# Two query buffers, loaded two tiles ahead, and a planner that counts 330 instead of 230 GB/s for transfers

## The chip, the cores and the metric

The kernel runs on one core of a Trainium2 chip. The metric is the device time of one execution in microseconds (us). The core has TensorE for matrix products (PE in the profile, its weight loads PEld), VectorE (DVE), ScalarE (ACT), GpSimd (POOL), and SyncE (SP), whose queue here issues nearly all DMA transfers. Each engine takes its own instructions strictly in the order in which the program was written out, and waits at the head of its queue until what it needs is there.

## What is computed

```python
# q, k, v: (4, 8, 576, 64); f: (4, 8, 576)
scores = q @ k.T / sqrt(64) + cum[:, :, :, None] - cum[:, :, None, :]   # cum = cumsum(log(clip(f)))
attn = softmax(where(causal, scores, -1e9)) @ v
x = attn as (2304, 512)
h = x @ w_in                                    # 512 x 1024
solu = h * softmax(h)
x = layernorm(solu) * g_ln @ w_out              # 1024 x 512
h = relu(x @ w2_in)                             # 512 x 2048
out = (h * h) @ w2_out                          # 2048 x 512
```

## The kernel before

**Precision.** Products are made from two halves: each float32 operand is split into a rounded part and a remainder (names ending in h and l), and three matmuls replace one.

**Attention with the first layer.** There are 20 query tiles (4 batches, 5 tiles each, of 128 or 64 rows). For each tile `load_k`, `load_q` and `load_v` fetch the rows from memory. `prep_k` and `prep_q` turn them into operands: for queries, three instructions for each of two halves j, on ACT, DVE or POOL (line 378, 380 or 384 for the scaled copies, line 541 on DVE for the remainder). The finished query operands Q1 and Q2 have two buffers, picked by tile number. The raw keys have two buffers KN (one for each half), the raw values six, and the raw queries one, `QN`, of 512 columns; a tile `q3` of 640 columns stands unused until the second layer's weights are put there. For each of 160 heads follow the scores (line 576, PE), the minimum (lines 594 and 597, DVE), the exponential (line 611, ACT), transposes (line 630, PE), their copies out (line 376 or another, by engine), and the product with the values (line 650). When a block of 128 tokens is complete, `first` runs the first layer on it (lines 869 to 950) and `out1` its second product (lines 820 to 822).

**Weights.** `convert` loads a piece of a weight as 64-bit words (line 715) and rebuilds float32 values with ACT, DVE and POOL (lines 729 to 747). The pieces of w_in are staged in four buffers, those of w_out in two (`xc` and `ws`). In `early2` the second layer's weights pass through five buffers called `free`, where they are converted and combined on POOL or DVE (lines 1098 and 1106), and are written to scratch memory: `w2d` (line 758), `w2u` (line 1101), `w2f` (line 1114). A buffer is used again only when its write has landed.

**Second layer.** `half_up` (line 1341), `unit` (line 1392) and `step` (lines 1497 to 1499) run the two big products. Their weights are read from the scratch memory by `within` (line 1168) and by `weights` in `unit` (line 1381).

**The order.** Nothing of this order is written by hand. `Plan.add` collects steps with a cost in ns for each engine that may run them, a due time (`prio`), and the buffers they read and write. `Plan.lay` then plays the program through at the time of building: a list scheduler with one server for each of PE, DVE, ACT and POOL, and one server called dma for all transfers. A transfer takes its stated cost on that server, one after the other, and then 1,410 to 1,790 ns until an engine sees it (`LAT`). At each point the scheduler takes what can start first, among those within 20 ns what is due first, and on engines other than PE it holds back for a more urgent step in some cases (`DUE`, `WORTH`). The order found is the order of the program; its times are not used on the chip, where each engine waits for what it needs. Costs in the code: 1,140 ns for 256 KB of queries, keys or values, 4.45 ns per column for a piece of a first-layer or raw second-layer weight (2,278 ns for 512 KB), 350 ns for the 16 KB rows of line 506, 570 ns for a write of 128 KB, `LOAD2` = 900 ns for 256 KB of the second layer's prepared weights. Where PE would wait for more than 400 ns in the first 140 us, `fill` puts transposes of no use there, so that TensorE's clock stays up (line 1706 in the trace).

In the loop over tiles the loads are added so (before):

```python
if h == PQ and n + 1 < NQ:        # PQ = 6
    prep_q(n + 1, when[s])
    if n + 2 < NQ:
        load_q(n + 2, when[s])
```

Of the kernel before, what the change touches and what calls it, by code (L numbers as in the profile page):

```python
# [27 lines left out]
class Plan:  # L28
# [11 lines left out]
        dve=dict(pe=230, dve=127, act=198, pool=203, dma=1230),  # L40
        act=dict(pe=110, dve=142, act=153, pool=160, dma=1234),
        pool=dict(pe=135, dve=75, act=75, pool=88, dma=1200),
        dma=dict(pe=1500, dve=1450, act=1410, pool=1450, dma=1790),
# [16 lines left out]
    def add(self, eng, fn, prio, reads=(), writes=(), take=None, uses=(), late=0, port=False, kind="r"):  # L60

        s = Step()
        s.eng, s.fn, s.prio, s.take, s.no, s.late = eng, fn, prio, take, len(self.steps), late
        deps = {}
        s.uses = tuple(uses) + ((take,) if take else ())
        for k in s.uses:  # L70
            self.users.setdefault(k, []).append(s)
        s.weak, s.port, s.kind = None, port, kind
        for k in reads:
            if k in self.writer:
                deps[self.writer[k].no] = self.writer[k]
            rs = self.readers.setdefault(k, [])
            if k in self.banks or k[0] in ("pp", "hp"):

                if rs and rs[-1].no not in deps:
                    s.weak = rs[-1]  # L80
                    deps[s.weak.no] = s.weak
            rs.append(s)
        for k in writes:
            if k in self.writer:
                deps[self.writer[k].no] = self.writer[k]
            for r in self.readers.get(k, ()):
                deps[r.no] = r
        for k in writes:
            self.writer[k] = s
            self.readers[k] = []  # L90
        deps.pop(s.no, None)
        s.deps = list(deps.values())
        s.succ = []
        for d in s.deps:
            d.succ.append(s)
        s.left = len(s.deps)
        s.rdy = {}
        s.end = None
        self.steps.append(s)
        return s  # L100
# [26 lines left out]
    def lay(self, slack=60):  # L127
# [53 lines left out]
        while todo:  # L181
            pick = None
            for e in engs:
                cand = []
                for s in avail[e]:
# [5 lines left out]
                    if e == "dve" and len(s.eng) > 1:  # L191

                        o = min(max(free[x], s.rdy[x]) + s.eng[x] for x in s.eng if x != e)
                        if t + s.eng[e] + SHIFT > o:
                            continue
# [73 lines left out]
def tile_kernel(ctx: ExitStack, tc: tile.TileContext, q, k, v, f, w_in, w_out, g_ln, w2_in, w2_out, out):  # L269
    nc = tc.nc  # L270
    NT, DM = out.shape
# [4 lines left out]
    P = 128  # L276
# [16 lines left out]
    HH = H // 2  # L293
# [17 lines left out]
    def new(tag, shape, dt=F32):  # L311

        tags[tag] = sb.tile([P] + list(shape), dt, tag=tag, name=f"{tag}_{len(tags)}")
        return tags[tag]
# [5 lines left out]
    woh, wol = (new(t, [KF, DM], F32R) for t in ("woh", "wol"))  # L320

    K2 = [new(f"k2{j}", [HH, KW], F32R) for j in range(2)]
    QN = new("qn", [DM])
    VN = [new(f"vn{i}", [DM]) for i in range(NV)]
    KN = [new(f"kn{i}", [DM]) for i in range(2)]
    pt = new("pt", [NPT * 5 * P])
# [4 lines left out]
    scratch = new("free", [5 * 768])  # L331
    new("ws", [768])
    new("xc", [768])
    new("q3", [640])
    new("xw", [256])
    ADJ = [new(f"adj{i}", [AW]) for i in reversed(range(NADJ))][::-1]
    ST = [new(f"st{i}", [2]) for i in range(NST)]
# [32 lines left out]
    def copy(n, dst, src, prio, reads, writes, uses=(), scale=None, psum=True, only=None):  # L370

        def fn():
            x = 1.0 if scale is None else scale
            if s.on == "act":
                if scale is None:
                    nc.scalar.copy(dst(), src())  # L376
                else:
                    nc.scalar.activation(out=dst(), in_=src(), func=AF.Copy, scale=scale)
            elif s.on == "pool":
                nc.gpsimd.tensor_scalar(out=dst(), in0=src(), scalar1=x, scalar2=1.0, op0=ALU.mult, op1=ALU.mult)  # L380
            elif scale is None:
                nc.vector.tensor_copy(dst(), src())
            else:
                nc.vector.tensor_scalar(out=dst(), in0=src(), scalar1=scale, scalar2=None, op0=ALU.mult)

        ap = not (scale is None or isinstance(scale, float))
        ns = dict(act=(51 if psum else 94) + 0.833 * n + (93 if ap else 0))
        ns["dve"] = 67 + 1.042 * n if psum else 68 + 0.522 * n + (61 if ap else 0)
        if not psum:
            ns["pool"] = (244 if ap else 161) + 0.833 * n  # L390
        if only:
            ns = {e: ns[e] for e in only}
        s = pl.add(ns, fn, prio, reads, writes, uses=uses, port=not psum)
        return s
# [10 lines left out]
    NQ = len(tiles)  # L405
# [22 lines left out]
    when = []  # L428
# [19 lines left out]
    def load_k(n, prio):  # L448
        T = tiles[n]
        m, o = T["m"], HH * T["q0"]  # L450
        for j in range(2):
            pl.add(
                dict(dma=1140 * m / P),
                lambda j=j: nc.sync.dma_start(KN[j][:, 0 : HH * m], k[T["b"], j, :, o : o + HH * m]), prio + 2 * j,
                writes=[("kn", j)],
            )

    def load_q(n, prio):
        T = tiles[n]
        m, o = T["m"], HH * T["q0"]  # L460
        pl.add(
            dict(dma=1140 * m / P), lambda: nc.sync.dma_start(QN[:, 0 : HH * m], q[T["b"], :, o : o + HH * m]), prio + 1,
            writes=["qn"],
        )

    def load_v(n, prio):
        b, t = tiles[n]["b"], tiles[n]["t"]
        vslot[b, t] = n % NV


        def fn():
            nc.sync.dma_start(VN[n % NV], v[b, t * P : t * P + P])

        pl.add(dict(dma=1140), fn, max(prio + 4, V0), writes=[("vn", n % NV)])
# [51 lines left out]
    def prep_q(n, prio):  # L526
        m = tiles[n]["m"]
        i = n % 2
        raw = QN[:, 0 : HH * m].rearrange("p (h s) -> p h s", s=m)
        for j, src in enumerate(own):  # L530
            q1, q2 = Q1[i][j], Q2[i][j]
            if n == 0 and j:
                prio = SECOND
            for rows, dst, nm in ((LO, q2, "qh"), (HI, q1, "qd")):
                copy(
                    HH * m, lambda rows=rows, dst=dst: dst[rows, :, 0:m], lambda src=src: raw[src], prio + 2 * j, ["qn"],
                    [(nm, i, j)], (), SC, False, None if n else ("act", "dve")[j:] if j else ("act",),
                )

            def lo(src=src, q1=q1, hi=(q1 if j else q2)):  # L540
                nc.vector.scalar_tensor_tensor(
                    out=q1[LO, :, 0:m], in0=raw[src], scalar=SC, in1=hi[src, :, 0:m].bitcast(F32), op0=ALU.mult,
                    op1=ALU.subtract,
                )

            pl.add(
                dict(dve=67 + 1.045 * HH * m), lo, prio + 2 * j, ["qn", ("qd" if j else "qh", i, j)], [("ql", i, j)],
                port=True,
            )

# [416 lines left out]
    def k_keys(nm, j):  # L967
        cs = ("kh",) if nm == "k1" else ("ka0", "ka1", "kl")
        return [c for y in cs for c in kcells(y, j, 0, KW)]

    held = {f"{nm}{j}": k_keys(nm, j) for nm in ("k1", "k2") for j in range(2)}
    for i in range(NV):
        held[f"vn{i}"] = [("vn", i)]
    for i in range(2):
        held[f"kn{i}"] = [("kn", i)]
        for j in range(2):
            held[f"q1{i}{j}"] = [("ql", i, j), ("qd", i, j)]
    held["qn"], held["q3"] = ["qn"], []
    for i in range(NADJ):
        held[f"adj{i}"] = [("adj", i, y) for y in range(2)]  # L980
    held["pt"] = [("pt", i, g) for i in range(NPT) for g in range(5)]
# [372 lines left out]
    def unit(b, p, prio):  # L1354
# [70 lines left out]
        prod(3, prio)  # L1425
        copy(TB, u2f, lambda: half(0), prio, [ks[0]], [uk], slots_of([ks[0]]))
        add(u2f, u2f, 1, prio, [], [uk])
        r1, r2 = new_r(*s1, prio), new_r(*s2, prio)
        c22, c12, c11, c21 = rof(*s2, 2, 2), rof(*s2, 0, 2), rof(*s1, 0, 2), rof(*s1, 2, 2)
        add(c22, u2f, 2, prio, [uk, "rqs"], [r2], (), r2)  # L1430
        add(c22, c22, 3, prio, [], [r2], [r2])
        prio += MID
        for i in (4, 5, 6):
# [122 lines left out]
    pl.add(dict(dma=350), sync(fl, f.rearrange("b h s -> (b h) s")), -9e6, [], ["f"])  # L1556
    load_k(0, -8e6)
    load_q(0, -8e6)
    load_v(0, -8e6)
    ones = E[0 : B * H, P : P + S]  # L1560
# [9 lines left out]
    for y, (a, e) in enumerate(((0, P), (P, S))):  # L1570
        w = slice(a, e)
        n = e - a
# [76 lines left out]
    for n in range(NQ):  # L1649
        for h in range(H):  # L1650
            s = n * H + h
            if h == 0 and n + 2 < NQ:
                load_v(n + 2, when[s])
            if h == PK and n + 1 < NQ:
                prep_k(n + 1, when[s])
                if n + 2 < NQ:
                    load_k(n + 2, when[s])
            if h == PQ and n + 1 < NQ:
                prep_q(n + 1, when[s])
                if n + 2 < NQ:  # L1660
                    load_q(n + 2, when[s])
            head(s)
            w = 4 if n >= QUADS else 2
            if (h + 1) % w == 0:
                mix(s, w)
        if tiles[n]["done"]:
            first(tiles[n]["x"])
# [9 lines left out]
    for x in ORDER:  # L1677
        nm, p = x[0], int(x[1])
# [10 lines left out]
    for b in range(1, NTB // 2 + 1):  # L1689
        for p in range(KP):  # L1690
            n = (b - 1) * KP + p
# [22 lines left out]

SHIFT = 650
XB = 1
AHEAD = 10000.0
V0, LOAD1 = -15000.0, 3000.0  # L1720
# [74 lines left out]
```

## Time and profile before

| | |
|---|---|
| time, median of 3 runs | 811.17 us (811.07 to 811.35) |
| profiled execution, span from first to last instruction | 811.2 us |
| PE busy | 790.8 us, 97% |
| PEld busy | 726.7 us, 90% |
| DVE busy | 638.9 us, 79% |
| ACT busy | 550.3 us, 68% |
| POOL busy | 384.6 us, 47% |
| moved by DMA | 159.69 MB, mean 197 GB/s |

The profiled execution has only its span of 811.2 us as a time of its own. Busy is the share of time in which an engine had an instruction in work; matmuls are pipelined and their ends are modelled, so a busy PE isn't a PE at its peak, and the filler transposes count as busy too.

### The profile page before, as it was taken

The page shows a single profiled execution, that of the slowest core. Times are in us where ns is not written, and L with a number is a line of the kernel's source. Part 1 is how long each engine was busy: PE and PEld are TensorE (multiplying, and loading weights), DVE is VectorE, ACT ScalarE, POOL GpSimd, SP SyncE. Part 2 cuts the span into 40 slices and gives each one's busy share as a digit, 9 for nine tenths or more (in the row PEclk, how much of TensorE's full clock was granted, in tenths as well). Part 3 has the DMA queues.
Part 4 walks back from the last instruction along what each step waited for, and adds up shares of the span by engine and source line. Part 5 has one row for each costly group of instructions (what it writes and reads, how often), then busy time and mean ns, then how long its engine had stood idle before and what let it go on. Part 6 is the DMA issues. An engine that isn't in the chain of part 4 may idle for free.

```text
span 811.2 us, 19134 instructions
## 1 busy us (share of the span) xinstructions
PE 790.8 (97%) x6607; PEld 726.7 (90%) x6607; DVE 638.9 (79%) x1627; ACT 550.3 (68%) x1425; POOL 384.6 (47%) x520
## 2 busy tenths in 40 slices
PE   7899999999999999999999999999999999999997
PEld 6677788888888888888989999999999999999997
DVE  8788788787786667886677879779778877987777
ACT  6899998889998888898886775445335343533442
POOL 6467778666778686777757622120211121112110
PEclk9999999999999999999999999999999999999999
DMA  6644346656664555665477899696767767675401
GB/s 216 206 117 140 105 128 186 206 173 190 199 206 163 189 171 165 196 229 180 169 247 232 265 309 368 213 321 212 229 207 233 230 203 223 216 232 186 159 1 53
DMA packets 109665, 159.69 MB, mean 197 GB/s; under 512 B 12832, under 2 KB 52768, under 8 KB 109568
## 3 DMA queue, kind: packets, MB, share of 16 engines
q1 hardware_dynamic: 109280, 158.21, 60.9%
q8 instruction: 52, 0.85, 0.4%
q14 instruction: 45, 0.37, 0.2%
q10 hardware_dynamic: 288, 0.26, 0.1%
HBM read 121.65 MB, written 36.72 MB: 195 GB/s over the span
## 4 chain that ended last, share of the span: by engine, by line
PE 47%; POOL 2%; DVE 2%; issue 1%; DMA 1%; ACT 1%; DVEq 0%; POOLq 0%
PE z L1392 9%; PE pp L1392 9%; PE hp L1497 4%; PE hp L1498 4%; PE hp L1499 4%; PE z L1341 3%; PE xo L1498 2%; PE xo L1499 2%; PE xo L1497 2%; DMA w2d<-free 1%; PE pp L1498 1%; PE pp L1499 1%; PE pp L1497 1%; PE pp L820 1%; PE pp L822 1%
## 5 line engine op out<-in xcount | busy, mean ns | idle before, releaser
L611 ACT ACTIVATE adj<-z,st 64x288 f32<-64x288 f32 (+9 forms) x192 | 95.0, 498 | 17.7 <-DVE st L597 15.9
L576 PE MATMUL z<-k,q 80*64 80x288 f32 (+17 forms) x384 | 89.9, 331 | 0.2
L597 DVE CUSTOM_DVE_ANT_0 z<-z,maskb 128x128 f32<-128x128 f32 (+8 forms) x144 | 65.3, 462 | 26.8 <-PE z L576 24.8
L630 PE MATMUL pp<-ident,adj 128*128 128x128 f32 (+1 forms) x480 | 76.4, 273 | 9.2 <-ACT adj L611 8.2
L821 PE MATMUL pp<-ln,wol 128*128 128x256 f32 x288 | 80.1, 278 | 0.0
L822 PE MATMUL pp<-ln,woh 128*128 128x256 f32 x288 | 80.1, 278 | 0.0
L630 PEld LDWEIGHTS pp<-ident,adj 128*128 128x128 f32 (+1 forms) x480 | 50.7, 140 | 32.4 <-ACT adj L611 22.4
L376 ACT COPY pt<-pp 128x384 f32<-128x384 f32 (+5 forms) x167 | 67.5, 422 | 15.2 <-PE pp L630 13.7
L1153 DVE TENSOR_TENSOR k<-adj,k 128x512 fp32r<-128x512 f32 (+1 forms) x71 | 48.9, 688 | 32.5 <-POOL k L380 25.2
L743 POOL TENSOR_TENSOR free<-free 128x256 uint32<-128x256 uint32 x64 | 49.1, 772 | 33.9 <-DVE free L737 20.7
L576 PEld LDWEIGHTS z<-k,q 128*128 128x128 f32 (+3 forms) x384 | 54.9, 176 | 8.3 <-ACT adj L611 4.1
L869 PE MATMUL hp<-wih,xl 128*128 128x512 f32 x144 | 60.0, 417 | 0.8 <-ACT hp L908 0.8
L650 PE MATMUL xo<-pt,vn 128*64 128x128 f32 (+1 forms) x960 | 60.4, 268 | 0.1
L650 PEld LDWEIGHTS xo<-pt,vn 128*64 128x64 f32 x960 | 48.6, 137 | 9.4 <-issue 5.4
L870 PE MATMUL hp<-wil,xh 128*128 128x512 f32 x144 | 56.6, 393 | 0.2 <-DVE wil L747 0.2
L871 PE MATMUL hp<-wih,xh 128*128 128x512 f32 x144 | 56.8, 394 | 0.0
L1106 POOL TENSOR_TENSOR free<-free 128x256 f32<-128x256 f32 x64 | 52.5, 821 | 7.5 <-DMA w2d<-free 4.8
L821 PEld LDWEIGHTS pp<-ln,wol 128*128 128x128 f32 x288 | 54.4, 189 | 0.4
L822 PEld LDWEIGHTS pp<-ln,woh 128*128 128x128 f32 x288 | 54.1, 188 | 0.0
L1098 POOL TENSOR_TENSOR free<-free 128x256 fp32r<-128x256 f32 x63 | 50.0, 805 | 7.4 <-ACT free L376 6.9
L380 POOL TENSOR_SCALAR k<-adj 128x512 fp32r<-128x512 f32 x37 | 23.1, 624 | 63.7 <-PE xo L1499 25.7
L1392 PE MATMUL z<-wol,k 128*128 128x256 f32 x384 | 52.4, 276 | 0.0
(614 smaller groups left out, 2682.4 us busy)
## 6 DMA issues: line engine op xcount, KB each, us to landing
k<-w2u SPq DMA_DIRECT2D x96, 256.0 KB
ln<-w2u SPq DMA_DIRECT2D x96, 256.0 KB
w2u<-free SPq DMA_DIRECT2D x56, 256.0 KB
kn<-in_k_dram SPq DMA_DIRECT2D x32, 256.0 KB
free<-in_moe_w_out_dram SPq DMA_DIRECT2D x32, 256.0 KB
free<-in_moe_w_in_dram SPq DMA_DIRECT2D x32, 256.0 KB
q<-w2u SPq DMA_DIRECT2D x32, 256.0 KB
w2f<-free SPq DMA_DIRECT2D x49, 128.0 KB
```

The costliest lines, as they stand in the source:

```text
L376: nc.scalar.copy(dst(), src())
L576: nc.tensor.matmul(dst, lhsT=ql[0:r, p, 0:m], rhs=rhs, start=(g == 0), stop=(g == 1))
L597: nc.vector.tensor_tensor_reduce(out=z, in0=z, in1=maskb[0:m, o : o + e - a], scale=1.0, scalar=st[0:m, 0:1] if y else 3e38, op0=ALU.add, ...
L611: nc.scalar.activation(out=adj[0:m, c[1] : c[2]], in_=Z[c[0]][0:m, 0 : c[2] - c[1]], func=AF.Exp, bias=st[0:m, low : low + 1], scale=-1.0, ...
L630: nc.tensor.transpose(at(sk)[:, (c - g) * m : (c - g + 1) * m], adj[0:m, zc : zc + P], ident[0:m, 0:m])
L650: nc.tensor.matmul(XO[own[j], g // 2, off : off + m], lhsT=VN[vslot[b, c]][:, (g + j) * D : (g + j + 1) * D], rhs=PT[(s - h + g + j) % NPT ...
L821: nc.tensor.matmul(px, lhsT=wol[:, fc, w], rhs=hi, start=False, stop=False)
L822: nc.tensor.matmul(px, lhsT=woh[:, fc, w], rhs=hi, start=False, stop=(fc == KF - 1))
L869: nc.tensor.matmul(HP[:, c], lhsT=XL[i][:, cc, :], rhs=wih[:, cc, w], start=(cc == 0), stop=False)
L871: nc.tensor.matmul(HP[:, c], lhsT=XH[i][:, cc, :], rhs=wih[:, cc, w], start=False, stop=(cc == KC - 1))
L1392: nc.tensor.matmul(half(i), lhsT=l, rhs=r[:, c * TB : c * TB + TB], start=(j == start), stop=(j == 5), skip_group_check=True,)
L1497: nc.tensor.matmul(po, lhsT=gl, rhs=wh, start=(p == 0 and i in opens), stop=False, skip_group_check=True)
```

## The change

Raw queries get a second buffer: the formerly unused `q3` tile, used for odd tiles, `qn` for even ones. The load for tile n + 2 is now added at the first head of tile n (it was at the seventh, behind `prep_q(n + 1)`), and needs only that the queries of tile n have been prepared. `q3` now has a holder, so second-layer weights can be put there only after the last odd tile's queries. And every cost on the planner's dma server is multiplied by `RATE` = 0.7: 256 KB of queries count as 798 ns, which is 328 GB/s instead of 230. The delays of `LAT` stay.

```diff
+        if "dma" in eng:
+            eng = dict(dma=eng["dma"] * RATE)
...
-    QN = new("qn", [DM])
+    QN = [new("qn", [DM]), new("q3", [640])]
...
-    new("q3", [640])
...
     def load_q(n, prio):
-            dict(dma=1140 * m / P), lambda: nc.sync.dma_start(QN[:, 0 : HH * m], q[T["b"], :, o : o + HH * m]), prio + 1,
-            writes=["qn"],
+            dict(dma=1140 * m / P), lambda: nc.sync.dma_start(QN[n % 2][:, 0 : HH * m], q[T["b"], :, o : o + HH * m]), prio + 1,
+            writes=[("qn", n % 2)],
...
     def prep_q(n, prio):
-        raw = QN[:, 0 : HH * m].rearrange("p (h s) -> p h s", s=m)
+        raw = QN[i][:, 0 : HH * m].rearrange("p (h s) -> p h s", s=m)
...
-    held["qn"], held["q3"] = ["qn"], []
+    held["qn"], held["q3"] = [("qn", 0)], [("qn", 1)]
...
             if h == 0 and n + 2 < NQ:
                 load_v(n + 2, when[s])
+                load_q(n + 2, when[s])
...
             if h == PQ and n + 1 < NQ:
                 prep_q(n + 1, when[s])
-                if n + 2 < NQ:
-                    load_q(n + 2, when[s])
...
-SHIFT = 650
+SHIFT, RATE = 650, 0.7
```

The reads in `prep_q` change from `"qn"` to `("qn", i)` as well.

## Rows read from the trace of the kernel before

**Rows 1.** Windows: from:to, length, busy of each engine, clock, DMA share, GB/s.
```profile
0.00:20.00 20.00, 14.72 (x95) 12.51 (x96) 16.25 (x36) 12.26 (x33) 12.84 (x23) 1.00 0.69 216
20.00:60.00 40.00, 36.32 (x282) 29.18 (x280) 33.66 (x74) 37.33 (x95) 20.52 (x19) 1.00 0.54 162
60.00:120.00 60.00, 58.51 (x463) 46.77 (x464) 47.80 (x119) 57.86 (x155) 43.99 (x65) 1.00 0.40 120
120.00:430.00 310.00, 304.71 (x2504) 263.07 (x2505) 235.40 (x637) 270.41 (x784) 227.54 (x300) 1.00 0.60 192
430.00:480.00 50.00, 50.00 (x411) 48.96 (x410) 40.41 (x73) 34.95 (x80) 26.66 (x29) 1.00 0.83 261
480.00:520.00 40.00, 40.00 (x354) 40.00 (x353) 33.60 (x79) 21.48 (x45) 6.10 (x10) 1.00 0.99 334
520.00:790.00 270.00, 269.94 (x2365) 269.73 (x2364) 216.47 (x571) 110.72 (x229) 46.92 (x80) 1.00 0.63 203
790.00:812.00 22.00, 16.63 (x147) 16.43 (x145) 15.31 (x44) 5.29 (x10) 0.00 (x0) 0.93 0.14 49
```

**Rows 2.** The same windows for the filler transposes alone (PE, PEld).
```profile
0.00:20.00 20.00, 9.79 (x61) 8.95 (x62) 1.00 0.69 216
20.00:60.00 40.00, 13.20 (x105) 11.54 (x103) 1.00 0.54 162
60.00:120.00 60.00, 5.19 (x44) 4.82 (x44) 1.00 0.40 120
```

**Rows 3.** Waits of PE and of POOL, 120 to 430 us: total us, times, longest.
```profile
PE pp L676 <- POOL x L380: 1.3, 1, 1.3
...
POOL free L1106 <- DMA w2d<-free: 4.8, 3, 2.4
```

**Rows 4.** The query buffer's instructions: idle time before them, by what ended it.
```profile
  DMA qn<-in_q_dram: 0.3, 1
```

**Rows 5.** SP's own waits up to 450 us.
```profile
SPq L462 <- DVE q L541: 20.9, 10, 6.0
```

**Rows 6.** Timelines of SP, POOL and PE: one query load, its preparation, its tile's scores.
```profile
122.32 0.36 SPq L462 DMA_DIRECT2D qn<-in_q_dram  x1
126.01 1.47 POOL L380 TENSOR_SCALAR q<-qn 64x512 fp32r<-64x512 f32 x2
139.94 0.84 PE L576 MATMUL z<-k,q 128*128 128x320 f32 x4
```

**Rows 7.** Timeline of SP at the start.
```profile
2.58 0.43 SPq L472 DMA_DIRECT2D vn<-in_v_dram  x1
5.11 3.06 SPq L506 DMA_DIRECT2D k<-xh  x4
8.21 0.44 SPq L715 DMA_DIRECT2D ln<-in_moe_w_in_dram  x1
```

**Rows 8.** Timelines of PE and POOL at the start; in brackets idle before and releaser.
```profile
8.28 0.73 PE L576 MATMUL z<-k,q 128*128 128x256 f32 x4
12.35 0.70 POOL L380 TENSOR_SCALAR ln<-ln 128x512 uint32<-128x512 uint32 x1 [3.50 <-DMA ln<-in_moe_w_in_dram]
```

**Rows 9.** Window of the busiest transfers at the start, columns as in rows 1.
```profile
10.00:20.00 10.00, 6.57 (x44) 4.39 (x43) 8.16 (x23) 6.47 (x24) 5.94 (x5) 1.00 0.93 303
```

**Rows 10.** Chain that ended last: start, us, the writes of w2d in it.
```profile
396.73 1.69 DMA w2d<-free
417.59 5.03 DMA w2d<-free
```

**Rows 11.** Timelines of POOL and PE about 423 us.
```profile
422.75 0.93 POOL L1106 TENSOR_TENSOR free<-free 128x256 f32<-128x256 f32 x1 [2.39 <-DMA w2d<-free]
423.65 1.05 POOL L380 TENSOR_SCALAR x<-su 128x512 f32<-128x512 f32 x1
424.76 0.66 PE L676 MATMUL pp<-ident,x 128*128 128x128 f32 x4 [1.33 <-POOL x L380]
```

**Rows 12.** Timeline of SP: the weight piece loaded into q3.
```profile
194.30 0.32 SPq L1168 DMA_DIRECT2D q<-w2f  x1
```

More of the change, by code (lines that the diff above doesn't have):

```diff
@@ L535, in prep_q @@
                 copy(
-                    HH * m, lambda rows=rows, dst=dst: dst[rows, :, 0:m], lambda src=src: raw[src], prio + 2 * j, ["qn"],
+                    HH * m, lambda rows=rows, dst=dst: dst[rows, :, 0:m], lambda src=src: raw[src], prio + 2 * j, [("qn", i)],
                     [(nm, i, j)], (), SC, False, None if n else ("act", "dve")[j:] if j else ("act",),
@@ L546, in prep_q @@
             pl.add(
-                dict(dve=67 + 1.045 * HH * m), lo, prio + 2 * j, ["qn", ("qd" if j else "qh", i, j)], [("ql", i, j)],
+                dict(dve=67 + 1.045 * HH * m), lo, prio + 2 * j, [("qn", i), ("qd" if j else "qh", i, j)], [("ql", i, j)],
                 port=True,
```

## The prediction

> **What bounds the kernel.** I read the windows first, then the fillers, then the waits, and last the timelines of the queues. The windows [rows 1] split the span of 811.2 us into three kinds of time. From 430 to 790 us PE is busy for 359.94 of 360 us: the second layer is bound by its matmuls, and nothing that starts earlier there can save anything. In the last window PE lacks some 4.6 us (21.2 us of the span are left in it, 16.63 busy); that is the chain of the last folds and writes, which the change touches only in the cost that the planner gives four writes. From 120 to 430 us PE idles 310 - 304.71 = 5.3 us. The first 120 us are different. PE idles 120 - 109.55 = 10.45 us there, and 28.18 us of its busy time are filler transposes [rows 2]: 38.6 us in which it does nothing that the result needs. So a gain can come from the first 120 us (38.6 us at most) and from the gaps after it (5.3 us), and since PE is full behind them, what is won there reaches the end almost whole. The clock plays no part: it is at 1.00 in every window but the last [rows 1], the upper of its two levels, and PE keeps it there with the fillers.
>
> What holds PE in the first 120 us is mostly ACT: 37.33 of 40 us busy from 20 to 60, 57.86 of 60 from 60 to 120. In the first 20 us ACT is busy only 12.26 us [rows 1], so 7.74 us of ACT lie open just where transfers are short.
>
> **Part 1, the queries.** Today the load waits for line 541, the last reader of the one buffer: 20.9 us of SP's waiting in ten pieces, the longest 6.0 us [rows 5]. The change ends these waits. What stood behind them in SP's queue were other transfers (rows of keys, writes of x2d and w2f). Does an engine wait for queries? Once, for 0.3 us, as counted at the instructions that use the buffer [rows 4]. In a tight case the load is issued at 122.32, used at 126.01, and the tile's first scores run at 139.94 [rows 6]: 13.9 us from prepared to needed, of which the remaining preparation takes part. The finished operands have two buffers already, so an earlier load can't make the preparation of tile n + 2 run before the scores of tile n are done. I price this part at 0, between a gain of 0.3 us (the one wait) and a loss of 0.3 us. The cover is the 13.9 us of lead; if it were gone in a tight tile, the 3.7 us from issue to use would show once.
>
> The load itself is moved past the value load and the key loads in the order of adding, and asks for its place 6 heads earlier; no instruction is added, and the same 20 issues stay. The cost on the other side is `q3`: its piece of weights is loaded at 194.30 today [rows 12] and can now come only after the last odd tile's queries, near 375 us. That leaves over 100 us until it is used. One 128 KB load and its two conversions move, and I count 0.
>
> **Part 2, the planner's rate.** This changes no transfer, only the order in which every engine does its work. Its largest sure effect is at the start. Before, the plan thinks the first four 256 KB loads (two of keys, one each of queries and values) and f busy until 350 + 4 x 1,140 = 4.9 us; by then the auxiliary rows of the keys (line 506) are ready, and being due first they go first. On the chip SP issues the value load at 2.58, waits for those rows, and issues the first piece of w_in only at 8.21 [rows 7]. With 0.7 the planned server is free at 0.7 x 4.91 = 3.4 us, before the rows can be ready (SP reaches them at 5.11), and an idle server takes what can start: one piece of w_in, planned at 1.6 us, perhaps two. The first piece can be issued right behind the value load, at 3.0 us: 5.2 us earlier. Today POOL sits idle for 3.50 us until that very piece has landed, at 12.35 [rows 8].
>
> What does this bring? At most the 5.2 us. At least it costs: 512 KB ahead of the rows take 0.52 MB / 303 GB/s = 1.7 us [rows 9], two pieces 3.5 us, by which the first scores, today at 8.28 [rows 8], would come later. The gain comes only if ACT and DVE use the time, and one piece gives them some two us of work each that now lies in the crowded stretch after 20 us. I take half of the bound, -2.6 us, with -5.2 and +3.5 as ends.
>
> The pieces of w_out go through two buffers, eight in each, and each planned turn gets 0.3 x 1,139 = 342 ns shorter: 2.7 us over eight turns at the most, at least 0. They run between 45 and 105 us, where ACT is full, so I take -0.5.
>
> From 120 to 430 us the shorter costs let the five buffers of the second layer's weights turn faster in the plan. The plan gives a w2d write 570 ns, which becomes 399, and 1,450 ns until POOL sees it. The chip took 1.69 us from issue to landing in one case and 5.03 in another [rows 10]. POOL waits for such writes 4.8 us in three pieces today [rows 3]; one of them, 2.39 us at 422.75, holds POOL so long that its next instruction, wanted by PE, is late, and PE waits 1.33 us [rows 11]. Other orders may close this gap (-1.3) or open more of the kind: if each of the three waits reached PE as that one did, 3 x 1.3 = 3.9 us would be lost. I take 0.
>
> The Trainium skill speaks against this part. "DMA: Bandwidth & Descriptors", in "Anatomy of one DMA", puts some 2 us on every transfer whatever its size, mostly for the receipt from memory, and in "Latency and other measured facts" lets the memory's latency rise from 0.2 to 2 us under load. The two landings in rows 10 are one size and differ by 3.3 us, which agrees. By that page the term of the writes would be a loss and no 0.
>
> **The sum.** 811.2 + 0 (queries) - 2.6 (start) - 0.5 (w_out) + 0 (second-layer weights) = 808.1 us, against a median of 811.17, which the profiled execution equals to 0.1 us. I predict 808.0 us.
>
> **Rivals.** *Hidden anyway, 811 us.* ACT is full from 20 us on [rows 1], so an earlier piece of w_in only moves a wait from POOL to ACT. For it: POOL and DVE have room in every window and still PE waits. Against it: ACT's 7.74 open us in the first 20. It would stay within 810 to 812.
>
> *The plan promises what transfers can't keep, 815 us.* The place is 430 to 520 us. The prepared weights are planned at 900 ns for 256 KB, 291 GB/s, and from now on at 630, 416 GB/s. At a DMA share of 0.99 the chip moved 334 [rows 1]. Today the plan is slower than the chip, so data are there first, and PE never waits. With 0.7 a plan that fills 40 us is ahead of the chip by 40 x (1 - 334 / 416) = 7.9 us at the end, and a matmul placed by it stands in front of all others in PE's queue. Against it: pieces are asked for more than 10 us ahead, and PE's work is ordered by due times as well. It decides once PE's waits there exceed the 3.1 us won before; I price it at half of 7.9, without the gain: 811.2 + 4 = 815. The page named above, in "Where 436 GB/s comes from", gives about 358 GB/s as what one core can draw from memory; 416 lies above that too, and the measured 334 agrees with it as a ceiling.
>
> *Writes behind POOL, 814 us.* The term left at 0 goes bad: +3.9 from the three waits and no more than 1 us won at the start, so 811.2 + 3.9 - 1 = 814. The point where it decides is three PE waits of 1.3 us behind POOL.
>
> *The start opens up, 801 us.* If a quarter of the 38.6 us without use falls to better order, 9.7 us are gained: 801.5. For it: that much is open. Against it: ACT is at 96% from 60 to 120 us.
>
> **How the numbers follow.** 808.0 and its neighbourhood (804 to 809.5) get 0.44, hidden anyway 0.20, the saturated stretch 0.15, writes behind POOL 0.14, the open start 0.07. The likeliest is 808.0. Its own ends are 811.2 - 5.2 - 2.7 = 803.3 and, with the start's loss, 814.7; the range runs from 801, the open start's edge, to 817, a little over the saturated stretch's 815 and under its full 819. Measurements of this kernel can tell 0.2%, 1.6 us: faster (under 809.5) 0.51, within 0.20, slower (over 812.8) 0.29.
>
> **What would show it.** In the profile after: the first piece of w_in issued near 3 us and not at 8.2; first scores later by one or two us; POOL's wait of 3.5 us for it gone; less filler than 28.2 us and less idle in the first 120 us; SP no longer waiting for line 541; the last scores and the start of `half_up` some 3 us earlier, and all after that shifted by as much. The prediction is wrong if PE shows idle time between 430 and 520 us, if POOL's waits for w2d, w2u or w2f writes grow above some 10 us and PE's waits behind POOL with them, or if ACT's idle time moves and the sum of filler and idle stays at 38.6.

## The result and the profile after

| | before | after |
|---|---|---|
| median of 5 runs | 811.35 us (811.07 to 813.23) | 825.12 us (820.44 to 827.35) |
| profiled execution, span | 811.2 us | 818.6 us, of a run of 820.44 us |
| PE, ACT, POOL busy | 790.8, 550.3, 384.6 us | 794.2, 548.0, 398.0 us |

The kernel became slower: ratio 1.0147 [1.0119, 1.0175]. The forecast of 808.0 us had the wrong sign, and its range ended at 817. In all runs that list both, the span lies 1.7 to 2.1 us below the time, so a span of 811.2 belongs to a run of about 813 us. The profiles compare an execution of before that was some 1.7 us above its median with one of after that was 4.7 us below it. They can show 7.4 us of the 13.8.

Windows of the kernel after, columns as in [rows 1] (lines of the source stand one higher than before, 577 for 576):

```profile
0.00:20.00 20.00, 14.09 (x80) 11.68 (x80) 15.48 (x32) 14.70 (x36) 10.49 (x21) 0.91 0.80 231
20.00:60.00 40.00, 37.97 (x283) 30.80 (x282) 32.48 (x76) 37.49 (x95) 20.61 (x18) 0.96 0.58 184
60.00:120.00 60.00, 56.27 (x458) 45.33 (x458) 48.77 (x117) 55.25 (x152) 44.24 (x63) 1.00 0.32 102
120.00:430.00 310.00, 302.54 (x2467) 259.79 (x2463) 232.37 (x628) 264.40 (x764) 236.28 (x316) 1.00 0.59 187
430.00:480.00 50.00, 49.70 (x418) 47.55 (x417) 39.04 (x71) 36.53 (x83) 29.43 (x34) 1.00 0.86 288
480.00:520.00 40.00, 39.54 (x337) 39.34 (x337) 30.07 (x66) 19.81 (x40) 7.56 (x13) 1.00 0.94 322
520.00:790.00 270.00, 270.00 (x2375) 270.00 (x2374) 219.48 (x573) 110.56 (x227) 48.75 (x81) 1.00 0.64 204
790.00:819.00 29.00, 24.05 (x213) 23.86 (x211) 21.79 (x62) 9.28 (x18) 0.62 (x1) 0.99 0.11 38
```

The same windows for the filler transposes alone, as in [rows 2]:

```profile
0.00:20.00 20.00, 9.43 (x55) 8.66 (x55) 0.91 0.80 231
20.00:60.00 40.00, 14.44 (x113) 13.14 (x113) 0.96 0.58 184
60.00:120.00 60.00, 5.73 (x46) 4.81 (x44) 1.00 0.32 102
```

Read the two together, stretch by stretch. In the first 120 us PE idles 11.67 us and fills 29.60: 41.3 us without use, 2.6 more than before [rows 1, 2]. Up to 60 us, where the clock is lower, it is as much as before (31.8 us against 31.9); from 60 to 120 us it is 9.5 against 6.7. From 120 to 430 us it idles 7.46 us instead of 5.29, 2.2 more. From 430 to 520 us it idles 0.76 us where it idled not at all. From 520 us on PE is full, as before, and the last window's loss (28.6 us of the span less 24.05) is the old 4.6 us. That makes 5.5 us; the clock, at 0.91 and 0.96 in the first two windows, is the only other difference in these rows. The loss has no single place: 4.8 of the 5.5 us lie ahead of 430 us, spread over the whole attention part.

The count of matmuls tells much the same without any model of their ends, though it takes large and small ones alike. Less the fillers, both traces hold 6,392 of them. PE had done 194 by 60 us (before 211), 606 by 120 us (before 630), by 430 us 61 fewer than before, by 520 us 70 fewer. The last scores start at 426.46 us (before 418.63) and `half_up` at 449.70 us (before 445.77); the prediction had both some 3 us earlier than before.

The start, timelines of SP, ACT, PE and POOL in the kernel after; in brackets idle time and what ended it:

```profile
3.06 0.43 SPq L716 DMA_DIRECT2D ln<-in_moe_w_in_dram  x1
4.86 3.15 SPq L507 DMA_DIRECT2D k<-xh  x4
...
9.37 0.69 ACT L730 ACTIVATE ln<-ln 128x512 f32<-128x512 f32 x1 [1.83 <-DMA ln<-in_moe_w_in_dram]
...
8.02 0.36 PE L577 MATMUL z<-k,q 128*128 128x256 f32 x1
9.06 0.63 PE L577 MATMUL z<-k,q 80*128 80x256 f32 x3 [0.67 <-DMA k<-xh]
...
12.74 1.48 POOL L499 TENSOR_TENSOR k<-kn,k 64x512 fp32r<-64x512 f32 x1 [3.29 <-ACT k L377]
```

The piece of w_in goes out at 3.06 and not at 8.21 [rows 7], and ACT has it in hand at 9.37, where POOL had it at 12.35 [rows 8]. So the plan's change did at the start what the prediction said. But three of the first four scores now wait for the key rows, and POOL's 3.50 us of waiting for that piece [rows 8] became 3.29 us of waiting for ACT, which has the piece's work ahead of a key's copy. The early piece moved a wait and saved nothing.

Waits in the kernel after: of POOL over the whole span, of PE from 120 to 430 us and from 430 to 520 us, of SP up to 450 us. Columns: total us, times, longest.

```profile
POOL free L381 <- DMA free<-in_moe_w_in_dram: 9.8, 11, 2.5
...
POOL free L1107 <- DMA w2d<-free: 1.1, 1, 1.1
...
PE pp L631 <- ACT adj L612: 4.3, 7, 1.4
...
PE z L1393 <- DVE ln1b L1419: 0.5, 1, 0.5
...
SPq L463 <- DVE q L542: 20.6, 12, 3.8
```

Two of the same waits in the kernel before, of POOL over the whole span and of PE from 120 to 430 us:

```profile
POOL free L380 <- DMA free<-in_moe_w_in_dram: 1.6, 2, 1.3
...
PE pp L630 <- ACT adj L611: 2.3, 6, 1.0
```

And in the kernel after the idle time at the instructions that use the query buffer `qn`, as in [rows 4]:

```profile
  DMA qn<-in_q_dram: 0.3, 1
```

Two buffers did not end SP's wait for the queries (20.6 us, before 20.9 [rows 5]), and no engine waited for queries beyond the old 0.3 us [rows 4]; the view of `q`, which takes in the odd tiles' buffer, shows no wait for that buffer's loads. PE's waits in the middle stretch are for the exponentials of ACT (2.3 us before, now 4.3), not for transfers or POOL.

### The profile page after: what moved, and what is told of

The parts are those of the page before. It is cut to its first block, busy times and chain, and to the rows that moved or that the text cites. A ratio compares the mean times of both kernels' runs of the same rounds, so it can differ in the third digit from the quotient of the medians.

```text
span 818.6 us, 19155 instructions
## 1 busy us (share of the span) xinstructions
PE 794.2 (97%) x6610; PEld 728.3 (89%) x6610; DVE 639.5 (78%) x1621; ACT 548.0 (67%) x1407; POOL 398.0 (49%) x544
## 4 chain that ended last, share of the span: by engine, by line
PE 52%; DVE 4%; DMA 1%; ACT 1%; issue 1%; POOL 0%; DVEq 0%; POOLq 0%; ACTq 0%
PE pp L1393 9%; PE z L1393 9%; PE hp L1499 4%; PE hp L1500 4%; PE hp L1498 4%; PE z L1342 3%; PE xo L1499 2%; PE xo L1500 2%; PE xo L1498 2%; PE xo L651 2%; PE pp L631 1%; PE pp L821 1%; PE pp L822 1%; PE pp L823 1%; PE pp L1499 1%; PE pp L1500 1%
## 5 line engine op out<-in xcount | busy, mean ns | idle before, releaser
L377 ACT COPY pt<-pp 128x256 f32<-128x256 f32 (+5 forms) x165 | 66.1, 421 | 16.7 <-PE pp L631 15.8
L744 POOL TENSOR_TENSOR free<-free 128x256 uint32<-128x256 uint32 x64 | 52.2, 822 | 22.7 <-DVE free L738 16.1
```

## The experiments

All kernels of a block ran on one chip with the kernel before. Some labels in the expectations: theory A puts the loss at the start, B in the cheaper transfers behind it, C in a redrawn order as such, D in the second query buffer, E in the second layer's weights being planned faster than they come. "Order" is always the order that the planner finds for all engines.

**1. The parts one at a time.** `q_only` has the two buffers and `RATE` 1.0; `rate_only` one buffer and `RATE` 0.7. `rate_start` is after with the rate for steps due in the first 60 us only, `rate_late` with the rate for all others:

```diff
-        if "dma" in eng:
+        if "dma" in eng and prio < 60000:     # rate_late: prio >= 60000
```

> Two query buffers and the early load alone, transfers planned at the old cost. Theory A (the loss is made in the first 60 us: the cheaper plan puts a 512 KB piece of w_in and a second query load ahead of the key rows that the first scores need, PE runs dry and its clock falls): 811 to 813, clock of the first 40 us at 1.00, no piece of w_in ahead of the key rows. Theory B (the loss is made from 60 us on, by plans for conversions that count on transfers which land later): 811 to 813 too. Theory C (any new order loses, since the order of before is a picked one): 814 to 824.

> One query buffer as before, every transfer planned at 0.7 of its cost. Theories A and B: the whole loss, 820 to 826. If the second query load at the start (8.0 us instead of 12.3) has a share in it, a few us less, 815 to 820. Theory C: anything between 812 and 826.

> Two query buffers; only transfers due in the first 60 us are planned at 0.7. Theory A: nearly the whole loss, 819 to 826, the clock down to half about 18 to 23 us as in the changed kernel. Theory B: 811 to 814. Theory C: 814 to 824.

> Two query buffers; only transfers due after the first 60 us are planned at 0.7. Theory A: 810 to 814, clock at 1.00 in the first 40 us. Theory B: 816 to 824, POOL waiting for raw weights some 10 us as in the changed kernel. Theory C: 814 to 824.

Measured: `q_only` 820.56 us, 1.0111 [1.0097, 1.0125]; `rate_only` 821.19, 1.0119 [1.0105, 1.0132]; `rate_start` 821.57, 1.0116 [1.0101, 1.013]; `rate_late` 822.56, 1.0153 [1.0127, 1.0179]. Each part alone costs 9 to 11 us, and the whole 14: they don't add up. `q_only` and `rate_late` plan the start at the old costs and lose as much, so the cheaper plan of the start isn't needed for a loss of this size. `q_only` and `rate_start` have the old costs behind it, so the later rate isn't needed either. The traces agree: up to 60 us PE is without use (idle or filler) for no longer in `q_only` (31.5 us) and `rate_late` (29.0) than in before (31.9). From 60 to 120 us it is for 13.7 and 13.2 us, against 6.7 in before, and `q_only`, which loses 7.0 us there, has a span only 7.5 us longer. But it isn't the common cause: `slack16` and `q_slack16` below lose there too (12.2 and 11.9 us), and are not as slow.

**2. Orders redrawn by numbers that mean nothing.** `nudge98` is the kernel before with every transfer planned 2% cheaper (`RATE` 0.98); `slack16` and `after_slack22` change `SLACK`, within which the scheduler prefers the earlier due time, from 20 to 16 ns in before, to 22 ns in after. `after_fill` gives after more filler, to hold the clock:

```diff
-SLACK = 20
+SLACK = 16        # slack16, in before; 22 in after_slack22
...
-WARM, GAP, SHARE, FILL = 140000.0, 400.0, 0.6, 62.0
+WARM, GAP, SHARE, FILL = 140000.0, 200.0, 0.75, 62.0     # after_fill
```

> One query buffer as before, every transfer planned at 0.98 of its old cost: a change of 23 ns in 1,140 with no meaning of its own, which only makes the planner write out another order. Theory C (the order of before is a picked one that runs some 8 us better than its like, and any new order loses that): 816 to 822. Theories A and B, and theory D (the two query buffers and the rate each do harm of their own): 810 to 813.

> The kernel before with the planner's window for choosing by due time at 16 instead of 20 ns; no transfer and no cost is changed. Theory C: 816 to 822. Theories A, B, D: 810 to 813.

> The changed kernel with that window at 22 ns. Theory C: another draw, 814 to 826, and not the same as the changed kernel's 825. Theory A: 820 to 826, since the start is planned as in the changed kernel.

> The changed kernel, its order kept, with more filler transposes in gaps of the first 140 us (from gaps of 200 ns on, and a share of 0.75 instead of 0.6), so that PE isn't idle between 8 and 20 us. If the fallen clock near 20 us is what separates the changed kernel's slow runs (827) from its fast ones (820) and is half of the loss: 815 to 820 and a narrow spread, clock at 1.00. If the clock is a side effect over filler time: 822 to 827 as before.

Measured: `nudge98` 820.95 us, 1.0106 [1.009, 1.0121]; `slack16` 815.42, 1.0045 [1.003, 1.006]; `after_slack22` 827.19, 1.0189 [1.0162, 1.0216]; `after_fill` 828.38, 1.0181 [1.0159, 1.0203]. A nudge of 2% costs 9 us, as much as either half of the change. Windows of `nudge98` up to 430 us:

```profile
0.00:20.00 20.00, 14.93 (x101) 12.46 (x102) 15.61 (x37) 13.31 (x36) 11.04 (x22) 1.00 0.67 211
20.00:60.00 40.00, 36.92 (x270) 28.96 (x269) 34.89 (x71) 37.40 (x95) 24.02 (x21) 0.96 0.59 177
60.00:120.00 60.00, 56.49 (x437) 45.10 (x436) 47.42 (x120) 53.35 (x146) 43.84 (x62) 0.98 0.36 110
120.00:430.00 310.00, 299.78 (x2441) 258.40 (x2442) 231.98 (x630) 264.10 (x765) 225.43 (x303) 1.00 0.59 187
```

and its filler transposes up to 120 us:

```profile
0.00:120.00 120.00, 23.88 (x182) 21.95 (x182) 0.98 0.49 149
```

The loss is as large as that of either half, with nothing but 2% in the costs, but it lies elsewhere. With 11.66 us idle and 23.9 us of filler, 35.5 us are without use up to 120 us, 3.1 fewer than in before; from there to 430 us PE idles 10.22 us, 4.9 more. The count of matmuls less fillers is 8 behind before at 120 us and 71 behind at 430 us. Idle time, filler and the lower clock of two windows (0.96 and 0.98, some 2.8 us) make up 4.6 of the 7.6 us by which the span is longer; the rest is longer busy time, and these rows don't show its cause.

The clock is not the common cause. `after_fill`, whose instructions other than filler stand in the order of after throughout, kept it at 1.00 from 0 to 120 us with 34.8 us of filler, and its span is 822.5 us, 3.9 longer than that of after; `rate_late` shows no fall either and is as slow. (`rate_start` lost some 12 us of clock in its first 130 us, counted as length times the share that the granted clock lacks of 1.00, the most of all; in that kernel it may matter.)

**3. The stretch of 430 to 520 us by itself.** `stretch430` is before with the rate for steps due from 430 us on. In its trace the transfers stand in the order of before up to 423 us and the engines' work up to 460. `after_load2` undoes the rate for the second layer's prepared weights alone; `shift600` and `nudge_late140` are two more redrawn orders of before: `SHIFT`, the advantage in ns from which DVE takes a step that another engine could do, 600 for 650; and 0.98 for steps due from 140 us on.

```diff
+        if "dma" in eng and prio >= 430000:      # stretch430, RATE 0.7; nudge_late140: 140000, RATE 0.98
+            eng = dict(dma=eng["dma"] * RATE)
...
-NPRE, LOAD2 = 1, 900
+NPRE, LOAD2 = 1, 900 / 0.7      # after_load2, in after
...
-SHIFT = 650
+SHIFT = 600      # shift600, in before
```

> One query buffer; only transfers due after 430 us are planned at 0.7, so that the order before 411 us (transfers) and 445 us (engines) is that of before, step for step. Theory E (part of the loss is made from 430 to 520 us, where the plan now counts on prepared weights sooner than they land): 812.5 to 816, PE idle 0.7 to 3 us from 430 to 520, first scores of the last tile where before has them. Theory C alone, without E: 811 to 813.5, PE idle under 0.3 there.

> The changed kernel with the prepared second-layer weights planned at their old cost (900 ns for 256 KB), all else at 0.7. Theory E: PE idle from 430 to 520 us back under 0.3 and the time from the start of the second layer to the end about 1 to 3 us shorter than in the changed kernel; the front is a new draw, so 817 to 823 in all, with a spread of runs of 3 us or less. Without E: idle stays at 0.7 to 3 us there, 820 to 827.

> The kernel before with another constant for the choice between DVE and the other engines, 600 instead of 650 ns; no transfer changed. Theory C: 814 to 822. Without C: 810 to 813.

> One query buffer; transfers due after 140 us planned at 0.98, so that the order up to about 127 us is that of before. Theory C with the advantage of before spread over the whole front: 814 to 818, about half of what the same nudge costs from the start (9 us). Theory C with the advantage in the first 120 us: 811 to 813. Theory C with the advantage behind 120 us: 818 to 822.

Measured: `stretch430` 813.53 us, 1.0027 [1.0013, 1.0041]; `after_load2` 820.32, 1.0096 [1.008, 1.0112]; `shift600` 813.79, 1.0025 [1.0014, 1.0036]; `nudge_late140` 817.75, 1.0071 [1.0055, 1.0087].

Windows of `stretch430` in the stretch:

```profile
430.00:480.00 50.00, 49.80 (x406) 48.55 (x405) 40.15 (x75) 34.89 (x78) 23.80 (x28) 1.00 0.88 283
480.00:520.00 40.00, 39.09 (x331) 38.34 (x331) 29.68 (x73) 16.98 (x36) 7.26 (x13) 1.00 0.92 315
```

Timelines of ACT, DVE and PE of the same kernel, whose lines stand two higher than those of before:

```profile
485.57 0.41 ACT L378 CAST xc<-xc 128x256 fp32r<-128x256 f32 x1 [2.30 <-DMA xc<-w2f]
...
490.25 0.35 ACT L378 COPY maskb<-pp 128x256 f32<-128x256 f32 x1
...
490.63 0.42 DVE L1420 TENSOR_TENSOR maskb<-maskb,pp 128x256 f32<-128x256 f32 x1 [0.90 <-ACT maskb L378]
...
491.10 0.95 PE L1394 MATMUL pp<-wol,ln 128*128 128x256 f32 x6 [0.58 <-DVE maskb L1420]
```

Here a plan was ahead of its data. At 485.57 ACT has waited 2.30 us for a weight piece; the copies behind it in its order are late, DVE waits 0.90 us for one of them, and PE 0.58 us for DVE. The way from the late piece to this PE wait over 5 us is read from the order, not traced row by row. In 480 to 520 us PE does 331 matmuls instead of 354 [rows 1], 23 fewer.

The 18 kernels divide cleanly by this. From 480 to 520 us PE idles in all six that plan the prepared weights at 416 GB/s (after 0.46 us, `stretch430` 0.91, `after_fill` 0.96, `rate_only` 1.31, `rate_late` 1.60, `after_slack22` 2.41), and not at all in the twelve that plan them at 291 GB/s, or 2% above. Ahead of that, from 430 to 480 us, idle time comes with either: 0.30 us in after, 1.12 in `rate_start`, behind the first layer and what feeds it.

**4. More draws, with one and two buffers, and the weights once more.** `q_shift600` and `q_slack16` are `q_only` (two buffers, old costs) with `SHIFT` 600 and with `SLACK` 16. `one_load2` is `rate_only` with `LOAD2` = 900 / 0.7, `load2_shift600` is `after_load2` with `SHIFT` 600.

```diff
-SHIFT, RATE = 650, 0.7
+SHIFT, RATE = 650, 1.0
...
-SLACK = 20
+SLACK = 16      # q_slack16, against after
```

> Two query buffers and the early load, all transfers at their old cost, the constant 600 instead of 650. With one buffer 600 gave 813.8. If the two buffers themselves do harm: 820 to 824, as far above 813.8 as their first order stood above before. If they are neutral and their first order was a bad draw: 813 to 818.

> Two query buffers and the early load, old costs, the planner's window at 16 ns. With one buffer 16 gave 815.4. Harm of the buffers: 821 to 825. Neutral: 813 to 818.

> One query buffer, all transfers at 0.7 but the prepared second-layer weights, which keep their old cost. Theory E says PE idles under 0.3 us from 430 to 520 us and that it gains 1 to 3 us on 821.2, the same with all transfers at 0.7: 817 to 820. If the cheaper transfers do no harm ahead of the second layer, it is a draw like the other orders at old costs: 812 to 818.

> The changed kernel with the prepared second-layer weights at their old cost, and 600 instead of 650. Another draw of 820.3: 814 to 824, PE idle under 0.3 us from 430 to 520 us. If the cheaper transfers do harm in the front by themselves, 818 to 824; if they don't, 813 to 818.

Measured: `q_shift600` 818.39 us, 1.0086 [1.0063, 1.0109]; `q_slack16` 809.58 us (808.73 to 810.72, 12 runs), 0.9973 [0.9964, 0.9982]; `one_load2` 819.05, 1.0087 [1.0071, 1.0102]; `load2_shift600` 820.16, 1.01 [1.0085, 1.0116].

Two buffers against one, each pair at the same numbers (medians of different blocks, whose medians of before lie within 0.5 us): 820.56 against 811.69 at 650 and 20 (8.9 slower), 818.39 against 813.79 at `SHIFT` 600 (4.6 slower), 809.58 against 815.42 at `SLACK` 16 (5.8 faster). The sign turns with a number that has nothing to do with queries. That the second buffer does harm is not shown, nor that it helps.

`one_load2` gives the cleanest size of the weights' part: its matmuls stand in the order of `rate_only` up to 458 us, and both begin the second layer at 448.52 us. The last part of the stretch in `rate_only`:

```profile
480.00:520.00 40.00, 38.69 (x326) 37.94 (x326) 29.82 (x67) 19.09 (x39) 7.07 (x12) 1.00 0.94 317
```

and in `one_load2`:

```profile
480.00:520.00 40.00, 40.00 (x351) 40.00 (x350) 29.91 (x70) 20.16 (x40) 8.65 (x15) 1.00 0.94 324
```

With the old cost PE idles no more and does 25 matmuls more, at some 0.11 us each 2.8 us; the spans differ by 818.3 - 815.7 = 2.6 us, the medians of the two blocks by 2.1. Only 1.31 us of it show as idle time. `after_load2` and `load2_shift600`, too, have no PE idle time between 430 and 520 us.

`q_slack16` is the version that beats both kernels, by 0.27% against before and 15.5 us (809.58 against 825.12) against after. Its windows:

```profile
0.00:120.00 120.00, 110.54 (x856) 91.95 (x857) 98.97 (x226) 106.71 (x279) 81.69 (x108) 1.00 0.49 150
120.00:430.00 310.00, 305.77 (x2542) 269.01 (x2541) 235.39 (x641) 267.63 (x780) 234.38 (x315) 1.00 0.61 193
430.00:520.00 90.00, 89.52 (x745) 88.18 (x745) 73.74 (x158) 53.97 (x118) 28.83 (x38) 1.00 0.88 292
```

PE idles 4.23 us from 120 to 430 us (before 5.29) and does 2,542 matmuls there, 38 more than before [rows 1]. Its start is no better than that of before: with 31.5 us of filler, 41.0 us of its first 120 are without use (before 38.6, after 41.3), and 626 matmuls are done by then (before 630, after 606).

## Why the prediction was wrong

**The step that failed is the sum.** It priced the places that the change names (start -2.6, w_out -0.5, queries 0, writes 0) and left the rest of the order as it stood in before. That order does not stand still: the planner decides every step from the times of all steps before it, and a changed cost redraws, from the first choice that it tips, all that follows on all engines. The page after shows it in the loads: POOL has 13.4 us more to do, ACT 2.3 us less. Eight orders at the old costs, or within 2% of them, some with a query part, were timed: `q_slack16` -0.27%, before 0, `shift600` +0.25, `slack16` +0.45, `nudge_late140` +0.71, `q_shift600` +0.86, `nudge98` +1.06, `q_only` +1.11. Their spread, 11 us, is larger than every term in the prediction, and before is the second best of the eight; after lies beyond all of them. Less the weights' part (below, some 0.3%) it stands just above their upper end. A forecast for a redrawn order should have begun near their mean, +0.5%, with a range of about 1% to either side. No rival said this. Three smaller slips: the prediction took the profiled execution for one of 811.2 us, and it was one of about 813; it called ACT full from 20 us on, and from 120 to 430 us ACT is busy for 270.41 of 310 us [rows 1], 87%; and it let the clock play no part, where after lost some 3.4 us of it ahead of 24 us (last section).

**Queries, 0 us.** As a wait, right: 0.3 us before and after. The piece of weights for `q3` went where the prediction said, from 194.3 to 376.4 us. Wrong that SP would no longer wait for line 541 (542 in after): it still does, for 20.6 us. As an edit to the plan it is a draw like the others, between 8.9 us slower and 5.8 us faster.

**Start, -2.6 us.** The mechanism was right (issued at 3.06 us, forecast 3.0; in an engine's hands 3 us earlier; three of the first four scores 0.8 us later, forecast one or two), the value wrong. What came free on POOL was lost again to a wait for ACT, and the time without use in the first 120 us rose by 2.6 us instead of falling. The rows of before showed ACT open in the first 20 us; that it is used now (14.70 us, before 12.26) did not carry past 60 us, where ACT does 55.25 us of work instead of 57.86. By 120 us ACT has worked for 107.4 us in both. The prediction had named "filler and idle stays at 38.6" as a sign that it is wrong; it was 41.3.

**w_out, -0.5, and the writes, 0.** No effect of either on PE is seen. POOL's waits for w2d writes fell (at the line of [rows 3] 4.8 us before, 1.1 after), so the rival "writes behind POOL" is out, and with it the loss for which the prediction called on the Trainium skill. The section that it names for the 2 us, "Anatomy of one DMA" in "DMA: Bandwidth & Descriptors", is headed for transfers that GpSimd issues, and these writes go out from SP. The 3.3 us between the two landings [rows 10] are more than the 1.8 us by which "Latency and other measured facts", the other section that it names, lets the memory's latency rise, so they don't bear it out. What grew is POOL's wait for the raw weights, 1.6 to 9.8 us over the whole span; PE's waits by the profile aren't behind those but behind ACT's exponentials.

**"The plan promises what transfers can't keep", 815 us.** The mechanism is confirmed by the three kernels with the old cost for the weights and by the division of the 18, the price was too high. The half of 7.9 us, 4 us, measured 2.1 us in median and 2.6 in span (`one_load2` against `rate_only`), and 0.27% [0.13, 0.41] or 1.1 to 3.3 us alone (`stretch430`). The prediction had named PE idle time between 430 and 520 us as a sign that it is wrong: after has 0.76 us there, 0.46 of it in this part. And 334 GB/s was no ceiling: in before itself, 10 us from 480 us on moved 367:

```profile
480.00:490.00 10.00, 10.00 (x90) 10.00 (x89) 9.01 (x17) 6.91 (x16) 2.85 (x5) 1.00 1.07 367
```

**What stays open.** Whether cheaper planned transfers harm the attention part by themselves: the three orders at 0.7 without the weights' part lie at +0.87, +0.96 and +1.00%, inside the eight but in their upper half. Too few draws tell that apart from chance. Second, why the median of after is 4.7 us above its profiled execution: the other four runs show a mean clock of 0.992 or 0.993 against 0.996, which is some 3 us of lower clock in 820 at most; no profile of such a run was taken. Which property makes one order better than another was not found either.

## What to carry to other kernels

When a list scheduler writes the order, a new cost or buffer is first of all a new draw: time a few null changes (2% in a cost, a tie rule) beside it, and count as its effect only what exceeds their spread or holds in several pairs. A picked order should be picked again after every such change; here, for the query buffers alone, that turned +1.1% (`q_only`) into -0.3% (`q_slack16`). And plan transfers no faster than the queue delivers where it is full: planning them at 416 GB/s cost 2 to 3 us there, and at 291 PE did not wait.

## What was not expected of the hardware

The granted clock fell to 0.50, the lower of its two levels, in the start of after; 2 us windows:

```profile
16.00:18.00 2.00, 1.27 (x8) 0.74 (x7) 1.97 (x7) 1.33 (x4) 1.31 (x2) 0.58 0.97 259
18.00:20.00 2.00, 2.00 (x9) 1.54 (x8) 0.88 (x1) 1.90 (x7) 0.34 (x1) 0.50 0.91 294
20.00:22.00 2.00, 2.00 (x11) 1.38 (x10) 1.44 (x5) 2.00 (x7) 0.00 (x0) 0.50 0.80 231
22.00:24.00 2.00, 2.00 (x15) 2.00 (x14) 1.45 (x4) 0.92 (x3) 1.47 (x1) 0.71 1.00 291
```

Ahead of it PE had been busy with gaps, 10.82 of the first 16 us. In `after_fill`, in the same order, it was busy for 11.17 of them, and there was no fall. Nor does the order settle it: in the first 400 us `stretch430` has the instructions of before in the order of before. In its first 12 us PE is busy for 8.69 us (before 8.92), and then its clock falls, where before shows 1.00 in the first 20 us [rows 1]:

```profile
12.00:14.00 2.00, 2.00 (x14) 1.54 (x12) 1.65 (x7) 2.00 (x7) 1.27 (x2) 0.67 0.82 238
14.00:16.00 2.00, 2.00 (x11) 1.33 (x9) 1.94 (x3) 1.05 (x5) 2.00 (x2) 0.50 0.95 349
```

By the four rows of after 3.4 us of clock were lost, and the same order with no loss (`after_fill`) was no faster. In `nudge_late140` the clock fell far from the start: 0.72 from 324 to 336 us, PE busy 10.40 of 12.

The transfers reached more than the 334 GB/s on which the rival's price rests, for 10 us, here in after:

```profile
500.00:510.00 10.00, 10.00 (x87) 10.00 (x86) 6.69 (x19) 2.96 (x6) 2.27 (x4) 1.00 1.03 373
```

With 373 in place of 334, the plan's lead over 40 us would be 40 x (1 - 373 / 416) = 4.1 us and half of it 2.1, as measured; but that is luck and no check, since over the whole 40 us after moved only 322 GB/s, and no row gives the half. The Trainium skill gives about 358 GB/s as a core's limit for transfers with memory ("DMA: Bandwidth & Descriptors", "Where 436 GB/s comes from"), which the prediction took for a ceiling; "HBM Reference", "Specifications (TRN2)", says that a core streaming alone goes well above its share. The 373 GB/s of this row agree with the second.
